# Attention and a routed mixture of experts on one core: the sums of k later, one of four probability copies on GpSimd, the pooled values' copy on ScalarE, and fewer copies for k's tail

## The chip, the cores and the metric

The kernel runs on one core of a Trainium2 chip. The metric is device time in microseconds (us): the median over runs of the kernel before is 694.59 us (three runs, 693.19 to 696.73). The engines named below are TensorE (PE in the profile, with its weight loads as PEld), VectorE (DVE), ScalarE (ACT), GpSimd (POOL) and SyncE (SP, which issues the plain loads and stores).

## The reference

Eight batches of eight heads, 576 positions of 64 numbers. Each head has two attentions that are added: a pooled one over sums of four neighbours (144 pooled positions), and a local one in which a position sees only those less than four away. The result, as 4,608 tokens of 512 numbers, goes through a router that picks one of eight experts for each token, and through that expert.

```python
q_d, k_d, v_d = (x.reshape(B, H, Sd, 4, D).mean(axis=3) for x in (q, k, v))
out_up = np.repeat(sm_attn(q_d, k_d, v_d), 4, axis=2)
mask = np.abs(pos[:, None] - pos[None, :]) < 4
attn = softmax(np.where(mask, scale * q @ k.T, -1e9))
x = rows_of(out_up + attn @ v)
logits = x @ w_gate + modality_bias[modality_id]
e = argmax(logits); gate = softmax(logits)[e]
out = gate * (relu(x @ w1[e]) @ w2[e])
```

The softmax's sums carry 1e-9 added.

## The kernel before

**Units.** Attention is cut into 32 units n, four to a batch; a unit is one pair of heads (g = n % 2 tells which half of a pair of units it is). Two units in sequence, an even and an odd one, share some work that is done once, with the even unit: the transposes of the last 64 positions of q and k (tpt), the pooled values (vp, vc), and the tails qT1, kT1 and kd1. So even units are the fuller ones. The steps of a unit, by the names that the text uses:

- tp (L275) and tpt (L288) transpose q and k on TensorE into PSUM. qT (L293, L295) and kT (L304, L305, L307) copy them on ScalarE into the tiles qT2 and kB, where kB has zeros around what belongs to the other head. kT1 are four copies of 64x64 for the tail of k.
- kd (L321, and L317 for the tail) sums four neighbours of k on VectorE, straight from the same PSUM tile that kT copies. qe and qd (L327, L331) do this for q on GpSimd in two steps.
- mk and sc (L341, L349) make the local scores on TensorE, window by window; lm and le (L356, L362) take their maxima and subtract them on VectorE; exp (L367) runs on ScalarE in place. scd (L376) makes the pooled scores, dm (L381) their maxima on VectorE, de (L389) their exponentials on ScalarE.
- z and zr (L393 to L399, VectorE) sum and invert; nl and nd (L403, L407, GpSimd) scale the two sets of probabilities.
- lt (L414, VectorE) transposes the local probabilities in blocks of 32; Pw_ (L419, ScalarE) copies them, in four copies of 32 partitions x 288 (Pw0 to Pw3), into a zeroed tile whose other columns stay zero. pdt (L428, TensorE) transposes the pooled ones and PdT (L436, ScalarE, two copies) takes them out of PSUM.
- vp makes the pooled values on TensorE and vc (L268) copies them on VectorE into the tile vd, once for two units. avd (L443) and avl (L458) are the products with the values, Od (L448, ScalarE) and X (L469, VectorE) scale and add them. For an odd batch, one copy on GpSimd (L1028) brings over the 64 positions left from the batch before it.

**Routing.** When the four units of batch b are through, its routing runs among the steps of unit 4b + 7: lg (L505), LT (L512) and lgt (L518) make the logits, L, ch1 and ch2 (VectorE, L524 to L555) find the expert, one-hot, and w is a small tile in that chain. pr (L570 to L574, TensorE) and pl turn it into places, which end in the tile si, and st (L615) scatters the tokens' numbers with GpSimd's indirect DMA, four scatters for an even batch and five for an odd one. For seven batches this lies in attention; the eighth is routed after it. In the last stretch of attention some weight preparation for the first expert joins in (whi L827, wlo L833).

**Order.** Nothing is reordered by a scheduler there. Each step has a number in the table PHASE, in units of one unit's time; a step of unit n is called at n + PHASE, steps of a batch at 4b + PHASE, and the sorted list of calls is emitted as it stands. So each engine's instructions are in that order, and each engine works through its own in turn, waiting where an operand isn't there. What two engines share is limited by PSUM tiles: the tag T (transposes tp, tpt, lgt, pdt, vp) has three buffers, S (scores) three, A (avl, avd, lg, pr) two.

**Experts.** From about 260 us on the experts' matmuls (L918, L966) run on TensorE, each f32 product made from three products of split numbers. Their order is set by a scheduler, and the eighth batch's routing lies at its beginning.

Of the kernel before, what the change touches and what calls it, by code (L numbers as in the profile page):

```python
# [7 lines left out]
F32 = mybir.dt.float32  # L8
# [14 lines left out]
SUB, WIN, KEYS = 24, 32, 30  # L23
BLK = 4 * SUB
NB = 6
PAD = 3
KT = S - SUB + WIN
# [17 lines left out]
NPW = 3  # L45
# [8 lines left out]

PHASE = {
# [22 lines left out]
class Consts:  # L78
    def __init__(s, tc, pool, psum):
        nc = tc.nc  # L80

        s.ps = psum
        pool.tile([128, 48], F32, name="pad")
        s.dummy = pool.tile([128, 128], BF16, name="dummy")
        nc.vector.memset(s.dummy, 0.0)
        s.busy(nc, 12)
        s.ident = pool.tile([128, 128], F32, name="ident")
        make_identity(nc, s.ident)
        s.identb = pool.tile([128, 128], BF16, name="identb")
        make_identity(nc, s.identb)  # L90

        x = pool.tile([128, 1], F32, name="warm")
        nc.vector.memset(x, 0.0)
        nc.scalar.activation(x, x, AF.Exp)
        m = pool.tile([128, WIN], BF16, name="band")
        nc.gpsimd.memset(m, 0.0)
        for j in range(4):
            t = m[32 * j : 32 * j + 32]
            nc.gpsimd.affine_select(out=t, in_=t, pattern=[[1, WIN]], compare_op=ALU.is_ge, fill=NEG, base=0,
                                    channel_multiplier=-1)  # L100
            nc.gpsimd.affine_select(out=t, in_=t, pattern=[[-1, WIN]], compare_op=ALU.is_ge, fill=NEG, base=6,
                                    channel_multiplier=1)
        s.mask = pool.tile([128, NB, WIN], BF16, name="mask")
        nc.vector.tensor_copy(s.mask, m.unsqueeze(1).broadcast_to([128, NB, WIN]))
        nc.vector.memset(s.mask[0:32, 0:2, 0:PAD], NEG)
        s.band = m

        s.pool = pool.tile([128, 32], F32, name="pool")
# [84 lines left out]
class Attention:  # L193


    def __init__(s, tc, ctx, ectx, C, psum, q, k, v):
        s.tc, s.C, s.ps = tc, C, psum
        nc = s.nc = tc.nc
        s.q, s.k, s.v = q, k, v

        s.ld = ectx.enter_context(tc.tile_pool(name="ald", bufs=2, side="right", reuse_waits="tile"))
        s.wk = ctx.enter_context(tc.tile_pool(name="awk", bufs=2, reuse_waits="tile"))
        s.one = ctx.enter_context(tc.tile_pool(name="aone", bufs=1, reuse_waits="tile"))
        s.QK, s.t = {}, {}
        s.vw = [(s.ld, s.one)[j].tile([128, H * NB, D], F32, name=f"vw{j}", bufs=1) for j in range(2)]

        s.qT2 = s.ld.tile([128, 2, S], F32, name="qT", bufs=1)
        s.kB = s.ld.tile([128, 2, 2, KT], F32, name="kT", bufs=1)
        nc.vector.memset(s.kB, 0.0)
        s.mask = s.one.tile([128, NB, WIN], BF16, name="mask")  # L210
        nc.vector.tensor_copy(s.mask, C.band.unsqueeze(1).broadcast_to([128, NB, WIN]))
        nc.vector.memset(s.mask[96:128, NB - 2 :, SUB + PAD : WIN], NEG)
        s.Pw = [s.one.tile([128, 2 * NB, 4, SUB], F32, name=f"Pw{j}") for j in range(NPW)]

        s.De = [s.one.tile([128, 3, 32 * NB], F32, name=f"de{j}") for j in range(3)]
        for j in range(2):
            (nc.vector, nc.gpsimd)[j].memset(s.vw[j], 0.0)

        for j in range(3):
            nc.vector.memset(s.De[j], 0.0)  # L220
# [44 lines left out]

    def vc(s, n, i):
        t = s.t["vd", n // 2] = s.wk.tile([96, 2, 4, D], F32, name="vd")
        s.nc.vector.tensor_copy(t, s.t.pop(("vp", n // 2)))  # L268

    def tp(s, n, nm):  # L270

# [25 lines left out]
    def kT_(s, n, i):  # L297
        g = n % 2
        p = s.t["tp", "t"][:, 1] if i else s.t["tp", "k", n]
        for a in range(2):  # L300
            r = slice(64 * a, 64 * a + 64)
            if i:
                t = s.kB[r].rearrange("m g a t -> m g (a t)")[:, :, KT * a + PAD : KT * a + PAD + 512 + 64]
                s.nc.scalar.copy(t[:, 0, 512:], p[r, :64])  # L304
                s.nc.scalar.copy(t[:, 1, :64], p[r, 64:])  # L305
            else:
                s.nc.scalar.copy(s.kB[r, g, a, PAD + 64 * g : PAD + 64 * g + 512], p[r])  # L307

# [107 lines left out]
    def Pw_(s, n, j):  # L416

        r = slice(32 * j, 32 * j + 32)
        s.nc.scalar.copy(s.Pw[n % NPW][r, :, j, :SUB], s.t["lt", n][r, :, :SUB])  # L419

    def pdt(s, n, i):

# [850 lines left out]
```

## Time and profile before

| | before |
|---|---|
| median of the runs (lowest, highest) | 694.59 us (693.19, 696.73; 3 runs) |
| profiled execution | 696.98 us: span 695.3, 1.7 around it |
| mean granted TensorE clock | 0.98 |
| TensorE busy | 649.5 us, 93% of the span |
| VectorE busy | 403.1 us, 58% |
| ScalarE busy | 379.9 us, 55% |
| GpSimd busy | 238.6 us, 34% |
| loads and stores (q1) | 86.71 MB, 53.9% of 16 DMA engines' span |
| GpSimd's indirect DMA (q0) | 19.18 MB, 8.6% |

The table's shares are averages over two different programs. Attention takes roughly the first 260 us of the span and keeps TensorE, VectorE, ScalarE and the DMA queues all well filled; the experts follow, and TensorE has no gap. In a row of the timeline the first number is the start in us from the beginning of the span, the second the duration in us, then engine, line, operation, output and inputs with their sizes; in square brackets is how long the engine sat idle before it and what ended that. Rows with x2 or x3 stand for so many instructions in a row. Instructions of one engine may overlap a little, the next one starting before the last one's record ends.

### The profile page before, as it was taken

The numbers are of one execution on the slowest core, as the hardware profiler recorded it, in microseconds if no ns is written. First come the engines' busy times: TensorE is split into PE (matmuls) and PEld (weight loads), VectorE is DVE, ScalarE is ACT, GpSimd is POOL, SyncE is SP. The second block draws the span as 40 slices with busy tenths as digits, with TensorE's granted clock in tenths as the row PEclk, the third lists the DMA queues.
The fourth block names the chain that finished last, engine by engine and source line by source line (L and its number), as shares of the span: only waits on it lengthen the run. The fifth ranks groups of instructions, "written<-read, shape, count | busy, mean of one in ns | idle before, by whom it ended". The sixth has DMA issues, their size and how long they took to land. (4 is left out here: it accounts for less than half of the span.)

```text
span 695.3 us, 16717 instructions
## 1 busy us (share of the span) xinstructions
PE 649.5 (93%) x6123; PEld 518.3 (75%) x6123; DVE 403.1 (58%) x938; ACT 379.9 (55%) x884; POOL 238.6 (34%) x302
## 2 busy tenths in 40 slices
PE   7898999888988889998999999999999999999896
PEld 4576666666656667886888888888888888889794
DVE  6688898888879886746444234323452343416610
ACT  4798998887888754452444334433443243425710
POOL 6644563635476564360220300403204012210111
PEclk9899999999999999999999999999999999999999
DMA  9899889998887938397561544616524345155700
GB/s 186 171 179 195 161 182 194 157 206 146 159 172 166 200 81 219 99 309 221 153 210 45 169 152 121 192 51 185 179 81 122 131 137 181 53 136 171 221 29 31
DMA packets 176423, 106.99 MB, mean 154 GB/s; under 512 B 136300, under 2 KB 154770, under 8 KB 176338
## 3 DMA queue, kind: packets, MB, share of 16 engines
q1 hardware_dynamic: 169138, 86.71, 53.9%
q0 software_dynamic: 7200, 19.18, 8.6%
q8 instruction: 50, 0.82, 0.5%
q14 instruction: 35, 0.29, 0.2%
HBM read 86.61 MB, written 19.51 MB: 153 GB/s over the span
## 5 line engine op out<-in xcount | busy, mean ns | idle before, releaser
L833 DVE TENSOR_TENSOR wlo<-raw,whi 128x1024 fp32r<-128x1024 f32 x73 | 87.9, 1227 | 79.6 <-ACT whi L827 72.4
L977 POOL DMA_INDIRECT out_dram<-o,tg x34 | 37.1, 1091 | 250.2 <-ACT o L969 194.6
L923 DVE SCALAR_TENSOR_TENSOR hl<-l,hh 128x512 fp32r<-128x512 f32 x72 | 49.5, 688 | 105.4 <-ACT hh L922 101.7
L922 ACT ACTIVATE hh<-l 128x512 fp32r<-128x512 f32 x72 | 42.6, 596 | 109.8 <-PE l L918 108.2
L966 PE MATMUL l<-whi,hh 128*128 128x512 f32 x256 | 100.2, 395 | 1.9 <-ACT hh L947 1.9
L966 PE MATMUL l<-whi,hl 128*128 128x512 f32 x256 | 99.9, 391 | 0.0
L966 PE MATMUL l<-wlo,hh 128*128 128x512 f32 x256 | 99.8, 391 | 0.0
L918 PE MATMUL l<-xh,whi 128*128 128x512 f32 (+1 forms) x256 | 95.1, 375 | 2.1 <-DVE hl L923 2.1
L918 PE MATMUL l<-xl,whi 128*128 128x512 f32 (+1 forms) x256 | 94.7, 370 | 0.0
L918 PE MATMUL l<-xh,wlo 128*128 128x512 f32 (+1 forms) x256 | 94.6, 370 | 0.0
L827 ACT CAST whi<-raw 128x1024 fp32r<-128x1024 f32 x70 | 71.5, 1051 | 29.6 <-DMA raw<-in_moe_w_dram 16.7
L969 ACT ACTIVATE o<-l,tg 128x512 f32<-128x512 f32 x37 | 25.4, 687 | 97.6 <-PE l L966 69.6
L403 POOL TENSOR_TENSOR le<-le,zr 128x384 f32<-128x384 f32 x32 | 26.6, 831 | 91.3 <-DVE zr L399 84.9
L966 PEld LDWEIGHTS l<-whi,hh 128*128 128x128 f32 x256 | 48.2, 188 | 11.8 <-ACT hh L947 2.2
L918 PEld LDWEIGHTS l<-xh,whi 128*128 128x128 f32 x256 | 48.1, 189 | 11.5 <-DVE hl L923 2.7
L419 ACT COPY Pw<-lt 32x288 f32<-32x288 f32 x128 | 54.5, 426 | 3.4 <-DVE lt L414 1.2
L966 PEld LDWEIGHTS l<-wlo,hh 128*128 128x128 f32 x256 | 48.2, 188 | 10.1
L966 PEld LDWEIGHTS l<-whi,hl 128*128 128x128 f32 x256 | 48.3, 189 | 9.5
L918 PEld LDWEIGHTS l<-xh,wlo 128*128 128x128 f32 x256 | 48.2, 188 | 8.3
L918 PEld LDWEIGHTS l<-xl,whi 128*128 128x128 f32 x256 | 48.3, 189 | 8.0
L896 DVE TENSOR_TENSOR xl<-xt,xh 128x512 fp32r<-128x512 f32 x37 | 24.3, 681 | 38.0 <-ACT xh L894 37.9
L615 POOL DMA_INDIRECT tab<-ig,si x36 | 38.5, 1068 | 20.7 <-DVE si L586 14.5
(245 smaller groups left out, 1297.7 us busy)
## 6 DMA issues: line engine op xcount, KB each, us to landing
raw<-in_moe_w_dram SPq DMA_DIRECT2D x176, 128.0 KB
raw<-in_moe_w_dram SPq DMA_DIRECT2D x44, 512.0 KB
vw<-in_v_dram SPq DMA_DIRECT2D x53, 180.0 KB
qt<-in_q_dram SPq DMA_DIRECT2D x30, 288.0 KB
kt<-in_k_dram SPq DMA_DIRECT2D x30, 288.0 KB
xs<-R SPq DMA_DIRECT2D x64, 128.0 KB
vw<-in_v_dram SPq DMA_DIRECT2D x15, 90.0 KB
xs<-R SPq DMA_DIRECT2D x12, 64.0 KB
```

The lines of the kernel that those rows point to most:

```text
L403: s.nc.gpsimd.tensor_tensor(e, e, z[:, : 2 * NB].unsqueeze(2).broadcast_to([128, 2 * NB, WIN]), op=ALU.mult)
L419: s.nc.scalar.copy(s.Pw[n % NPW][r, :, j, :SUB], s.t["lt", n][r, :, :SUB])
L615: i = nc.gpsimd.indirect_dma_start(out=s.tab[:, :], out_offset=bass.IndirectOffsetOnAxis(ap=C.si[:, t : t + 1], axis=0), in_=C.ig[:, t, :] ...
L827: (nc.gpsimd.tensor_copy if turn <= 4 else nc.scalar.copy)(hi, raw)
L833: (nc.gpsimd if turn == 4 else nc.vector).tensor_tensor(lo, raw, hi.bitcast(F32), op=ALU.subtract)
L896: nc.vector.tensor_tensor(xl[:, :, hs], p, xh[:, :, hs].bitcast(F32), op=ALU.subtract)
L918: nc.tensor.matmul(p[:, f % n, :], a[:, fs], x[:, k, :N], start=(k == 0 and i == 0), stop=(k == 3 and i == 2))
L922: nc.scalar.activation(hh[:, g, :N], p, AF.Relu)
L923: nc.vector.scalar_tensor_tensor(hl[:, g, :N], p, 0.0, hh[:, g, :N].bitcast(F32), op0=ALU.max, op1=ALU.subtract)
L966: nc.tensor.matmul(p, a[:, f, hs], x[:, f % 2, :], start=(f == 0 and i == 0), stop=(f == 7 and i == 2))
L969: nc.scalar.mul(o, p, T[:, h, 1:2].bitcast(F32))
L977: nc.gpsimd.indirect_dma_start(out=s.out[:, :], out_offset=bass.IndirectOffsetOnAxis(ap=T[:, h, 0:1], axis=0), in_=o, in_offset=None, boun ...
```

## The change

Four edits, all in attention:

1. kd0, the sums over the main 512 positions of k on VectorE, is called at phase 0.5095 in place of 0.3000. The steps between the two phases now come before it.
2. Of the four copies Pw_, the first (j = 0, partitions 0 to 31) is made by GpSimd, and it is called at 2.6300 in place of 2.7494: behind nd and, in the routing units, among the scatters.
3. vc, the copy of the pooled values out of PSUM, is made by ScalarE in place of VectorE, at 2.7495 in place of 2.6555.
4. The tail of k (kT1) takes two copies of 64x2x64 instead of four of 64x64. For that the tile kT becomes flat and 80 numbers longer, 2,416 a partition, so that the two halves of the tail lie at a constant distance; kB is a view of it, and its zeroing at the start is as much longer.

```diff
-    "kT1": 0.5356, "sc0": 0.5591, "qe": 0.6232, "qd": 0.6242, "lm0": 0.7343, "le0": 0.8414, "kd0": 0.3000, "kd1": 0.5400,
+    "kT1": 0.5356, "sc0": 0.5591, "qe": 0.6232, "qd": 0.6242, "lm0": 0.7343, "le0": 0.8414, "kd0": 0.5095, "kd1": 0.5400,
...
-    "nd": 2.5956, "vc": 2.6555, "Pw0": 2.7494, "pdt0": 2.7884, "PdT0": 2.9335, "PdT1": 2.9345,
+    "nd": 2.5956, "vc": 2.7495, "Pw0": 2.6300, "pdt0": 2.7884, "PdT0": 2.9335, "PdT1": 2.9345,
...
-        s.kB = s.ld.tile([128, 2, 2, KT], F32, name="kT", bufs=1)
-        nc.vector.memset(s.kB, 0.0)
+        s.kF = s.ld.tile([128, 4 * KT + 80], F32, name="kT", bufs=1)
+        nc.vector.memset(s.kF, 0.0)
+        s.kB = s.kF[:, : 4 * KT].rearrange("m (g a t) -> m g a t", g=2, a=2)
...
-        s.nc.vector.tensor_copy(t, s.t.pop(("vp", n // 2)))
+        s.nc.scalar.copy(t, s.t.pop(("vp", n // 2)))
...
-                t = s.kB[r].rearrange("m g a t -> m g (a t)")[:, :, KT * a + PAD : KT * a + PAD + 512 + 64]
-                s.nc.scalar.copy(t[:, 0, 512:], p[r, :64])
-                s.nc.scalar.copy(t[:, 1, :64], p[r, 64:])
+                t0, w = KT * a + PAD + 512, 2 * KT - 512
+                t = s.kF[r, t0 : t0 + 2 * w].rearrange("m (g t) -> m g t", g=2)
+                s.nc.scalar.copy(t[:, :, :64], p[r].rearrange("m (g t) -> m g t", g=2))
...
-        s.nc.scalar.copy(s.Pw[n % NPW][r, :, j, :SUB], s.t["lt", n][r, :, :SUB])
+        (s.nc.scalar.copy if j else s.nc.gpsimd.tensor_copy)(s.Pw[n % NPW][r, :, j, :SUB], s.t["lt", n][r, :, :SUB])
```

What each engine is given in its turn shows best side by side. The lines of the changed kernel are one higher from L210 on. VectorE in unit 7, the first with routing, before:

```order
L321 TENSOR_REDUCE kd<-tp 128x128
L356 TENSOR_REDUCE lm<-sc 128x6
L362 TENSOR_TENSOR le<-sc,lm 128x192
L524 TENSOR_REDUCE L<-lgt 128x16 x2
L531 TENSOR_TENSOR L<-L,tb 128x32
L533 TENSOR_REDUCE mx<-L 128x4
L534 TENSOR_TENSOR L<-L,mx 128x32
L414 STREAM_TRANSPOSE lt<-le 128x384
L381 TENSOR_REDUCE dm<-scd 128x3
L545 TENSOR_SCALAR w<-L 128x32
```

and now:

```order
L357 TENSOR_REDUCE lm<-sc 128x6
L363 TENSOR_TENSOR le<-sc,lm 128x192
L525 TENSOR_REDUCE L<-lgt 128x16 x2
L532 TENSOR_TENSOR L<-L,tb 128x32
L534 TENSOR_REDUCE mx<-L 128x4
L535 TENSOR_TENSOR L<-L,mx 128x32
L415 STREAM_TRANSPOSE lt<-le 128x384
L382 TENSOR_REDUCE dm<-scd 128x3
L322 TENSOR_REDUCE kd<-tp 128x128
L546 TENSOR_SCALAR w<-L 128x32
```

kd has moved from ahead of a score's maxima, past the logits, lt and dm, to a place just ahead of w. In units without routing it passes lm, le, lt and dm in the same way.

GpSimd in the second of the units that hold the scatters of batch 1, before (Pw_163 and the like are the three tiles that units take in turn, de_167 and de_168 those of the pooled probabilities):

```order
L615 DMA tab<-ig,si 41472x2
L407 TENSOR_TENSOR de_167<-de_167,zr 128x18x24
L327 TENSOR_TENSOR qe<-qT 128x288
L615 DMA tab<-ig,si 41472x2
L331 TENSOR_TENSOR qd<-qe 128x144
L615 DMA tab<-ig,si 41472x2
L403 TENSOR_TENSOR le<-le,zr 128x384
L615 DMA tab<-ig,si 41472x2
L407 TENSOR_TENSOR de_168<-de_168,zr 128x18x24
```

and now:

```order
L616 DMA tab<-ig,si 41472x2
L408 TENSOR_TENSOR de_167<-de_167,zr 128x18x24
L328 TENSOR_TENSOR qe<-qT 128x288
L616 DMA tab<-ig,si 41472x2
L332 TENSOR_TENSOR qd<-qe 128x144
L420 COPY Pw_164<-lt 32x12x24
L616 DMA tab<-ig,si 41472x2
L404 TENSOR_TENSOR le<-le,zr 128x384
L616 DMA tab<-ig,si 41472x2
L408 TENSOR_TENSOR de_168<-de_168,zr 128x18x24
```

One copy has come in, behind qd and ahead of two scatters, le and de.

ScalarE in an even unit, before:

```order
L293 ACTIVATE qT<-tpt 128x128
L448 ACTIVATE Od<-avd 128x144
L304 COPY kT<-tpt 64x64
L305 COPY kT<-tpt 64x64
L304 COPY kT<-tpt 64x64
L305 COPY kT<-tpt 64x64
L367 ACTIVATE le<-le 128x384
L419 COPY Pw_165<-lt 32x12x24
L389 ACTIVATE de_166,z<-scd,dm 128x6x24 x3
L436 COPY PdT<-pdt 96x2x144 x2
```

and now:

```order
L294 ACTIVATE qT<-tpt 128x128
L449 ACTIVATE Od<-avd 128x144
L306 COPY kT<-tpt 64x2x64 x2
L368 ACTIVATE le<-le 128x384
L269 COPY vd<-vp 96x512
L390 ACTIVATE de_166,z<-scd,dm 128x6x24 x3
L437 COPY PdT<-pdt 96x2x144 x2
```

The four small copies are two, and where Pw0 stood, the copy of the pooled values stands. In an odd unit Pw0's place is empty. TensorE's order doesn't change.

## The prediction

> **What bounds the kernel now.** I began with busy times by stage (the windows view), since an average over the whole run would mix two programs. Columns: the stretch, its length, then busy time of TensorE, its weight loads, VectorE, ScalarE, GpSimd, granted clock, DMA share, GB/s.
>
> ```profile
> 180.00:200.00 20.00, 18.87 (x396) 14.38 (x396) 18.54 (x58) 18.89 (x62) 12.40 (x16) 1.00 0.87 163
> 160.00:165.00 5.00, 2.84 (x65) 2.25 (x65) 4.97 (x13) 2.47 (x9) 4.55 (x6) 1.00 1.02 129
> 165.00:170.00 5.00, 4.41 (x51) 2.59 (x51) 4.33 (x17) 4.05 (x11) 2.59 (x4) 0.66 0.91 166
> 219.50:224.10 4.60, 3.87 (x95) 2.88 (x92) 4.39 (x13) 4.33 (x12) 4.17 (x7) 1.00 0.63 63
> 400.00:500.00 100.00, 100.00 (x458) 82.92 (x457) 39.55 (x45) 38.59 (x53) 19.36 (x18) 1.00 0.50 153
> ```
>
> In 400 to 500 us, the experts, TensorE is busy 100.00 of 100, so nothing the change does to other engines can shorten that stage; but what attention gains or loses moves all of it, whole. In 180 to 200, attention, TensorE, ScalarE and VectorE are each busy over 18.5 of 20: three engines share the bound. So the waits come next, over 40 to 245 us: engine and line, what they waited for, us in total, times, longest.
>
> ```profile
> POOL le L403 <- DVE zr L399: 73.8, 20, 8.2
> DVE kd L321 <- ACT kT L307: 13.0, 12, 2.2
> ...
> PE pdt L428 <- POOL de L407: 5.4, 8, 1.9
> ...
> PE tp L275 <- ACT PdT L436: 3.4, 8, 1.4
> ...
> ACT le L367 <- DVE le L362: 2.9, 3, 1.2
> PE avl L458 <- ACT Pw L419: 2.6, 5, 0.6
> ```
>
> TensorE waits little: for ScalarE 3.4 + 2.6 = 6.0 us, for GpSimd 5.4. The first two rows are idle time of engines that are not late. The timeline tells which engine closes the ring of a unit. Here is an odd unit without routing, ScalarE, then TensorE (start, duration, engine, line, operation).
>
> ```profile
> 67.91 0.69 ACT L436 COPY PdT<-pdt 96x288 f32<-96x288 f32 x2 [0.18 <-ACT de L389]
> ...
> 69.11 1.18 ACT L307 COPY kT<-tp 64x512 f32<-64x512 f32 x2
> 70.31 1.31 ACT L419 COPY Pw<-lt 32x288 f32<-32x288 f32 x3
> ...
> 72.39 0.41 ACT L419 COPY Pw<-lt 32x288 f32<-32x288 f32 x1
> ...
> 73.91 0.69 ACT L436 COPY PdT<-pdt 96x288 f32<-96x288 f32 x2
> ```
> ```profile
> 71.67 1.21 PE L458 MATMUL avl<-Pw,vw 128*64 128x96 f32 x24 [0.59 <-issue]
> ...
> 73.28 0.54 PE L428 MATMUL pdt<-ident,de 64*96 64x64 f32 x12
> ```
>
> From PdT to PdT it is 6.0 us, and the ring runs PdT, qT, kT, three Pw copies, then TensorE's avl, sc, pdt, which ends at 73.82, and PdT again at 73.91. The Pw0 copy at 72.39 lies beside TensorE's part. In an even unit ScalarE has no gap at all:
>
> ```profile
> 122.00 0.20 ACT L304 COPY kT<-tpt 64x64 f32<-64x64 f32 x1
> ...
> 122.67 0.52 ACT L367 ACTIVATE le<-le 128x384 f32<-128x384 f32 x1
> 123.10 0.42 ACT L419 COPY Pw<-lt 32x288 f32<-32x288 f32 x1
> 123.53 0.38 ACT L389 ACTIVATE de<-scd,dm 128x144 f32<-128x144 f32 x1
> ...
> 124.61 0.69 ACT L436 COPY PdT<-pdt 96x288 f32<-96x288 f32 x2
> ```
>
> **The change, part by part.** Prices first: busy time and mean ns of the groups, then the one GpSimd copy of the trace.
>
> ```profile
> L307 ACT COPY kT<-tp 64x512 f32<-64x512 f32 x64 | 37.0, 578 | 1.0
> ...
> L321 DVE TENSOR_REDUCE kd<-tp 128x128 f32<-128x512 f32 x32 | 21.5, 671 | 17.1 <-ACT kT L307 17.0
> ...
> L293 ACT ACTIVATE qT<-tpt 128x128 f32<-128x128 f32 x16 | 4.4, 277 | 2.4 <-PE tpt L288 2.0
> ...
> L1028 POOL COPY X<-late 128x256 f32<-128x256 f32 x4 | 1.6, 395 | 0.0
> ```
>
> *Even units, ScalarE.* Pw0 leaves: 123.53 - 123.10 = 0.43 off. The vd copy (96x512) comes: the kT copy, also 512 wide out of PSUM, lasts 0.578, and two follow each other in 1.18 (69.11), so I take 0.59. The four small kT copies took 122.67 - 122.00 = 0.67; two copies of 64x128 replace them, nearest to qT's 0.277 each. Those two kT copies, to different partition halves, did not overlap, so I take 0.57 for both, 0.10 off. Sum +0.59 - 0.43 - 0.10 = +0.06 a unit, x 16 = +0.96. If the new copies overlapped as well as the old (0.36 for two) it would be -0.15 a unit; if they saved nothing, +0.16: -2.4 to +2.6.
>
> *Odd units, ScalarE.* Pw0's 0.4 goes, but TensorE's pdt still ends at 73.82, so PdT can start only 73.91 - 73.82 = 0.09 earlier; and for the handing over I leave 0.03 of it: 0.06. Nine odd units carry no routing (16 less 7): -0.54. This is where most of the change's apparent gain stays behind.
>
> *The sums of k (kd), VectorE.* They move from ahead of a unit's score maxima to behind dm. 17.1 us of idle stood before them, most of it for kT, but VectorE's wait is no one's end except where something late is queued behind it: in the three places where ScalarE's exp waits for le (2.9 us) kd's 0.67 no longer stands ahead; I credit 3 x 0.65 = -1.95, bounds 0 and -2.9. In the seven units that carry a batch's routing the new place is worse. VectorE, then TensorE and ScalarE, of the first:
>
> ```profile
> 55.84 0.69 DVE L321 TENSOR_REDUCE kd<-tp 128x128 f32<-128x512 f32 x1 [1.25 <-ACT kT L307]
> ...
> 57.10 0.34 DVE L524 TENSOR_REDUCE L<-lgt 128x16 f32<-128x64 f32 x2
> ...
> 58.53 0.57 DVE L381 TENSOR_REDUCE dm<-scd 128x3 f32<-128x432 f32 x1
> 59.02 0.16 DVE L545 TENSOR_SCALAR w<-L 128x32 f32<-128x32 f32 x1
> ```
> ```profile
> 56.25 0.44 PE L518 MATMUL lgt<-ident,LT 128*128 128x128 f32 x2 [0.88 <-ACT LT L512]
> ...
> 60.72 0.18 PE L570 MATMUL pr<-oh,tri 128*128 128x32 bf16 x1 [0.43 <-DVE X L469]
> ```
> ```profile
> 61.62 0.60 ACT L295 ACTIVATE qT<-tp 128x512 f32<-128x512 f32 x1 [0.55 <-PE tp L275]
> ```
>
> From dm on the chain is tight: w, then X; TensorE's pr has waited 0.43 for X, its transposes (tp) follow, and ScalarE's qT has waited 0.55 for those. kd inside this chain costs 0.65. What it gives back ahead: L could start when lgt ends, 56.69, plus a handing over, near 56.8 instead of 57.10, so 0.3. Net +0.35, x 7 = +2.45; bounds 0.3 and 0.65, +2.1 to +4.5.
>
> In even units kd also stands before the small sums (L317), whose buffer the next pdt takes. I price it at nothing, because ScalarE has no gap there until 124.61; without that cover it would be up to 0.2 a unit.
>
> *Pw0 on GpSimd.* By elements, 395 x 288 / 256 = 0.44 us; no row shows a copy on 32 partitions. Pw0 waits for lt, and behind it stand the routing scatters and the next nl. Where GpSimd idles, that costs nothing: nl (L403) waits for zr,
>
> ```profile
> 69.80 0.83 POOL L403 TENSOR_TENSOR le<-le,zr 128x384 f32<-128x384 f32 x1 [0.66 <-ACT kT L307]
> ...
> 126.80 0.83 POOL L403 TENSOR_TENSOR le<-le,zr 128x384 f32<-128x384 f32 x1 [0.85 <-DVE zr L399]
> ```
>
> 0.66 to 0.85, about 0.75, even beside scatters, in the four even batches. In an odd batch (1, 3, 5) with its five scatters, the second unit's chain has no slack:
>
> ```profile
> 224.17 0.54 PE L428 MATMUL pdt<-ident,de 64*96 64x64 f32 x12 [0.22 <-POOL de L407]
> ```
>
> From 219.5 to 224.1 (first table) GpSimd is busy 4.17 of 4.60 in seven instructions one behind the other, two of them scatters, and TensorE's pdt waits for the last of them, de. Pw0 slips in between and is paid in full, 3 x 0.44 = +1.32. The other side: up to 1.05 each, the second rival.
>
> The Trainium skill speaks against this part ("GPSIMD Engine Reference", section 1, Specifications): GpSimd shares its SBUF interfaces with VectorE, and contends with VectorE instructions that have two SBUF inputs. The trace bears it out once (two pieces of the timeline, then all 32 qe: shortest, median, longest ns):
>
> ```profile
> 232.47 1.56 DVE L833 TENSOR_TENSOR wlo<-raw,whi 128x1024 fp32r<-128x1024 f32 x1
> ...
> 232.91 1.64 POOL L327 TENSOR_TENSOR qe<-qT 128x288 f32<-128x288 f32 x1
> ```
> ```profile
> L327 POOL TENSOR_TENSOR qe<-qT x32: 662/666/1641, 10.7 to 237.3; 128x288 f32<-128x288 f32 x32
> ```
>
> By that rule a Pw0 that met such an instruction would be stretched too, which is the second rival's time; by the median of qe, which is within 0.01 of the shortest, the sum's 1.32 stands.
>
> *Sum.* +0.96 - 0.54 - 1.95 + 2.45 + 1.32 = +2.2. The profiled execution, 696.98 (695.3 of span), becomes 699.2; it lies 2.4 above the median of 694.59, which becomes 696.8.
>
> **The rivals.** *ScalarE alone sets the pace, and the change is faster.* Over a pair of units ScalarE sheds 2 x 0.43 + 0.10 and takes 0.59, net -0.37, x 16 = -5.9; about as much as TensorE's waits for ScalarE, 6.0, which would all go: 694.6 - 6.0 = 688.6. For it: ScalarE's 18.89 of 20 and its gapless even unit. Against it: pdt's end at 73.82 in the odd ring, and VectorE's 18.54. Chance 0.25.
>
> *GpSimd's copy is slow, and the change is slower.* The qe above took 1.64 against 0.67 elsewhere when it ran beside VectorE's two-input wlo, 2.46 times as long. At that ratio Pw0 takes 0.44 x 2.4 = 1.05. Odd batches pay 3 x 1.05, and the four even ones what exceeds their slack, 4 x (1.05 - 0.75): 3.15 + 1.2 = 4.35 in place of 1.32, sum +5.3, so 699.9. It decides from about 0.8 us per copy, where 0.9 + 3p + 4(p - 0.75) passes 3.5. For it: this row. Against it: only one of 32 qe was stretched so. Chance 0.15.
>
> *The clock.* In 160 to 165 TensorE was busy 2.84 of 5, and in the next 5 us it was granted 0.66, which cost (1 - 0.66) x 5 = 1.7. The moved waits can add such a dip or remove one: 2.2 + 1.7 or 2.2 - 1.7, 698.5 or 695.1. Chance 0.10.
> By the Trainium skill ("TensorE: Matmul & The Clock Gate", Part 1, The HAM clock gate) the clock falls only after an idle window of about 3.4 us; by that no dip could come here, and this rival would be nothing. The trace does not agree: the dip follows 5 us that were more than half busy.
>
> **How the numbers follow.** The forecast has 0.50. A change of under 0.5% (3.5 us) is about what a measurement of this kernel can't tell from none. Faster by more, below 691.1: nearly all of the first rival and a little of the forecast's low tail, 0.24. Slower by more, above 698.1: of the second rival 0.13, of the clock 0.04, and of the forecast 0.12, since its terms reach from -2.4 to +2.6 on ScalarE and to +4.5 on VectorE; 0.29. The same: 0.47. The range goes up to 700.5, past the second rival, leaving 0.04 above. Down to 689.5 it takes in a third of the first rival, leaving 0.16 below: together 0.20.
>
> **What would show it.** Right: in odd units pdt still ends just before PdT, and TensorE's waits for PdT stay near 3; the vd copy shows 0.59 on ScalarE, the new kT copies 0.28, Pw0 on GpSimd 0.44; in routing units pr's wait for X grows by about 0.35; in odd batches pdt waits longer for GpSimd's de. Wrong: the waits for PdT and Pw fall near zero and the attention stage ends 5 us sooner (first rival), or Pw0 on GpSimd lasts over 0.8 (second).

## The result and the profile after

| | before | after |
|---|---|---|
| median (lowest, highest; runs) | 695.74 us (691.58, 698.22; 9) | 698.81 us (695.95, 703.52; 9) |
| ratio to before, 95% interval | | 1.0065 [1.0038, 1.0092] |
| profiled execution (span) | 696.98 us (695.3) | 697.65 us (696.0) |

The ratio is +4.5 us on 695.7, with an interval of +2.6 to +6.4 (the two medians lie 3.1 apart); the forecast was +2.2. The two profiled spans lie only 0.7 apart, in part because the clock dipped four times between 160 and 660 us in before's and once in after's; so they are compared below stage by stage.

Attention first. The waits from 40 to 245 us in the changed kernel (us in total, times, longest):

```profile
POOL le L404 <- DVE zr L400: 54.9, 15, 6.8
...
PE pdt L429 <- POOL de L408: 7.5, 8, 3.2
...
PE lgt L519 <- ACT LT L513: 6.3, 7, 1.1
...
PE pr L571 <- DVE X L470: 3.2, 4, 0.8
...
ACT le L368 <- DVE le L363: 3.1, 3, 2.3
PE avl L459 <- ACT Pw L420: 3.1, 5, 0.7
...
PE pr L571 <- DVE late L470: 2.8, 3, 0.9
...
PE tp L276 <- ACT PdT L437: 0.3, 1, 0.3
```

and three of the kernel before:

```profile
PE lgt L518 <- ACT LT L512: 5.2, 6, 0.9
...
PE pr L570 <- DVE X L469: 1.7, 4, 0.4
...
PE pr L570 <- DVE late L469: 1.4, 3, 0.5
```

VectorE's wait of 13.0 us with kd on kT is gone from the list: kd now comes so late that kT is always there. TensorE's wait for PdT fell from 3.4 to 0.3, and yet attention is not shorter, as the units below show. pr's waits for X and late together rose from 3.1 to 6.0 over seven routings, 0.41 each. The prices, by line:

```profile
L420 POOL COPY Pw<-lt 32x288 f32<-32x288 f32 x32 | 14.4, 449 | 8.4 <-DVE lt L415 8.3
L269 ACT COPY vd<-vp 96x512 f32<-96x512 f32 x16 | 9.3, 580 | 0.7 <-PE vp L264 0.4
L306 ACT COPY kT<-tpt 64x128 f32<-64x128 f32 x32 | 8.2, 258 | 0.4
```

What a unit costs is best read from one mark. "Ring n" is here the time from the first PdT copy (L436, L437 in the timeline) of unit n - 1 to that of unit n. Where nothing near it was changed, a ring repeats to within 0.02 us from kernel to kernel (ring 13 is 7.87 or 7.88 in all fourteen profiles), unless a clock dip or a gap falls into it in which TensorE waited for nothing that the profile shows; so a few hundredths are real. In us (e1 and so on are the experiments below):

| ring | before | after | Pw0 alone (e3) | vd alone (e6) | kd alone (e8) | after, kd early in routing units (e2) | after, four tail copies (e12) |
|---|---|---|---|---|---|---|---|
| 8 (even; 12, 16 alike) | 6.70 | 6.76 | 6.42 | 7.18 | 6.70 | 6.76 | 6.88 |
| 9 (odd) | 8.20 | 8.20 | 8.20 | 8.20 | 8.20 | 8.20 | 8.20 |
| 11 (odd batch) | 6.18 | 6.74 | 6.56 | 6.00 | 6.32 | 6.74 | 6.74 |
| 14 (routing) | 7.23 | 7.66 | 7.26 | 7.71 | 7.70 | 7.37 | 7.76 |
| 19 | 8.90 | 6.99 | 8.91 | 8.04 | 7.48 | 6.98 | 7.00 |
| 22 (routing) | 7.23 | 7.66 | 7.27 | 7.54 | 7.60 | 7.37 | 7.77 |

Rings 6 to 27 add up to 159.65 us before and 160.65 after, +1.0 (each from a profile in which it was undisturbed: before or e1; after, and for 23 to 25 e2). As profiled the sums are 164.86 and 163.85: a clock dip and several such gaps fall into before's, a gap of 1.65 us into after's, and they fall elsewhere in other executions. So the +1.0 rests on that choice of profiles. Units 28 to 31 are not in that sum: there GpSimd's whi waits for a weight load, 1.8 us before and 2.2 after, but 0.9 in e2, and that moves from one execution to the next.

The experts are the other place. VectorE at their beginning, before and then after; si holds the places of the last batch's tokens, and GpSimd's scatters wait for it:

```profile
281.58 0.19 DVE L585 TENSOR_REDUCE sf<-sl 128x5 f32<-128x40 f32 x1
281.85 1.23 DVE L833 TENSOR_TENSOR wlo<-raw,whi 128x1024 fp32r<-128x1024 f32 x1
...
283.22 0.16 DVE L586 CAST si<-sf 128x5 int32<-128x5 f32 x1
284.16 1.22 DVE L833 TENSOR_TENSOR whl<-raw,whl 128x1024 fp32r<-128x1024 f32 x1 [0.79 <-issue]
285.31 0.68 DVE L923 SCALAR_TENSOR_TENSOR hl<-l,hh 128x512 fp32r<-128x512 f32 x1
```
```profile
281.82 0.19 DVE L586 TENSOR_REDUCE sf<-sl 128x5 f32<-128x40 f32 x1
282.83 1.23 DVE L834 TENSOR_TENSOR whl<-raw,whl 128x1024 fp32r<-128x1024 f32 x1 [0.82 <-ACT whl L828]
...
284.20 0.68 DVE L924 SCALAR_TENSOR_TENSOR hl<-l,hh 128x512 fp32r<-128x512 f32 x1
284.80 0.16 DVE L587 CAST si<-sf 128x5 int32<-128x5 f32 x1
```

The scheduler has put whl and hl ahead of si. The first expert's matmuls began at 258.10 before and at 256.09 after, so si went from 25.1 to 28.7 us behind them. In all kernels with this order TensorE's and ScalarE's turn with VectorE's: the four transposes xt behind lgt come 11.2 us after the first matmul before (269.30) and, with 12 of the expert's matmuls now ahead of them, 14.5 after (270.56); on ScalarE an hh now stands ahead of a whi. So "order" below means all three together; no run here separates them. Also, the first scatter behind si now lasts twice as long, begun 0.14 us after a whl on VectorE (285.10), where before it began 0.51 us ahead of one:

```profile
283.65 1.03 POOL L615 DMA_INDIRECT tab<-ig,si  x1 [14.50 <-DVE si L586]
```
```profile
285.24 2.12 POOL L616 DMA_INDIRECT tab<-ig,si  x1 [17.37 <-DVE mn L749]
```

Behind si stand the five scatters, then the gathers (xg) and a store of results (out_dram) in GpSimd's queue; that store frees a buffer "o" for which VectorE waits, by after's row, at the head of its queue, with a weight product (wlo) behind it. GpSimd and VectorE before:

```profile
302.57 1.31 POOL L977 DMA_INDIRECT out_dram<-o,tg  x1 [0.30 <-issue]
```
```profile
310.05 0.42 DVE L652 TENSOR_TENSOR o<-ltri,mn 128x256 f32<-128x256 f32 x1 [4.45 <-issue]
310.51 0.42 DVE L654 TENSOR_REDUCE mincl<-o 128x16 f32<-128x256 f32 x1
310.85 1.21 DVE L833 TENSOR_TENSOR wlo<-raw,whi 128x1024 fp32r<-128x1024 f32 x1
```

and after:

```profile
305.81 1.04 POOL L978 DMA_INDIRECT out_dram<-o,tg  x1 [0.30 <-ACT whi L828]
```
```profile
314.06 0.43 DVE L653 TENSOR_TENSOR o<-ltri,mn 128x256 f32<-128x256 f32 x1 [6.99 <-DMA out_dram<-o,tg]
...
315.63 1.22 DVE L834 TENSOR_TENSOR wlo<-raw,whi 128x1024 fp32r<-128x1024 f32 x1
...
318.12 0.69 DVE L924 SCALAR_TENSOR_TENSOR hl<-l,hh 128x512 fp32r<-128x512 f32 x1
318.72 0.14 DVE L769 TENSOR_SCALAR rcnt<-rcnt 128x1 f32<-128x1 f32 x1
```

So wlo lies 52.8 us behind the first matmul before, and 59.5 after. For before's o the profile names no releaser. TensorE waits at that place; after's long wait is put down to rcnt, which follows the hl of 318.12 on VectorE. TensorE's idle time from 295 to 326 us, before and after,

```profile
319.05 0.50 PE L918 MATMUL l<-xh,whi 128*128 128x512 f32 x1 [0.47 <-DVE hl L923]
...
323.88 0.50 PE L918 MATMUL l<-xh,whi 128*128 128x512 f32 x1 [1.59 <-DVE hl L923]
```
```profile
312.20 0.50 PE L919 MATMUL l<-xh,whi 128*128 128x512 f32 x1 [0.91 <-ACT whi L828]
...
318.86 0.52 PE L919 MATMUL l<-xh,whi 128*128 128x512 f32 x1 [3.26 <-DVE rcnt L769]
```

is 2.1 and 4.2 us, and right behind the longer wait the clock falls (the second row: 3.4 us at 0.50, worth 1.7):

```profile
300.00:325.00 25.00, 20.83 (x87) 16.61 (x86) 12.88 (x21) 11.88 (x15) 11.69 (x11) 0.93 1.04 307
319.20:322.60 3.40, 3.40 (x10) 2.63 (x9) 1.89 (x3) 0.90 (x2) 0.00 (x0) 0.50 1.02 307
```

### The profile page after: what moved, and what is told of

It is laid out like the page before. It is cut to its first block, busy times and chain, and to the rows that moved or that the text cites. A ratio compares the mean times of both kernels' runs of the same rounds, so it can differ in the third digit from the quotient of the medians.

```text
span 696.0 us, 16656 instructions
## 1 busy us (share of the span) xinstructions
PE 641.6 (92%) x6123; PEld 512.7 (74%) x6123; DVE 394.4 (57%) x922; ACT 374.8 (54%) x836; POOL 251.8 (36%) x334
## 5 line engine op out<-in xcount | busy, mean ns | idle before, releaser
L970 ACT ACTIVATE o<-l,tg 128x512 f32<-128x512 f32 x37 | 25.3, 686 | 97.7 <-PE l L967 62.4
L404 POOL TENSOR_TENSOR le<-le,zr 128x384 f32<-128x384 f32 x32 | 26.6, 831 | 67.5 <-DVE zr L400 61.5
L459 PE MATMUL avl<-Pw,vw 128*64 128x96 f32 x768 | 39.2, 250 | 6.4 <-ACT Pw L420 3.8
```

The lines of the kernel that those rows point to most:

```text
L404: s.nc.gpsimd.tensor_tensor(e, e, z[:, : 2 * NB].unsqueeze(2).broadcast_to([128, 2 * NB, WIN]), op=ALU.mult)
L459: s.nc.tensor.matmul(p[64 * a : 64 * a + 64, c], vw[:, NB * (4 * (hp // 2) + hp % 2 + 2 * a) + k, :], Pw[:, 2 * k + a], start=True, stop=T ...
L970: nc.scalar.mul(o, p, T[:, h, 1:2].bitcast(F32))
```

## The experiments

Ratios are to runs of before on the same chip, with their 95% interval; 1% is 6.9 us. Theory A came out of the two traces: about half of the loss is in the experts, through the order that the scheduler chose there. The order turned out to be fickle: kd's move alone gives it, vd's move alone gives it, Pw0 and the tail copies don't, and even kd late in the single unit 5 does.

**e1: before, with the experts in the order of after.**

```diff
-                        call(n + p, values if f == "X" else getattr(at, parts.get(f, f)), n, i)
+                        call(n + (0.5095 if nm == "kd0" and n == 5 else p), values if f == "X" else getattr(at, parts.get(f, f)), n, i)
```

> The kernel before, with kd later in unit 5 alone. In attention that touches one unit, but it turns the scheduler's order on VectorE at the start of the experts into the one that the changed kernel has: the cast to si (the places of the last batch's tokens) comes behind one more weight product (whl) and one more hl. Theory A (about half of the change's loss lies in the experts, by this order): si and the scatters behind it come 2 to 4 us later against the first expert's matmuls, TensorE's gap near 319 us grows from 2.1 to about 4, and the time is 2 us above before. Rival B (all of the loss lies in attention): si moves, but the gap and the time stay as before, within 0.5 us.

1.0041 [1.0012, 1.0070], +2.8 us. si came 27.4 us behind the first matmul, and TensorE's waits from 295 to 325 us were 4.6:

```profile
PE l L918 <- DVE rcnt L768: 3.1, 1, 3.1
PE l L918 <- DVE hl L923: 1.0, 1, 1.0
PE l L918 <- ACT o L969: 0.5, 1, 0.5
```

Attention's rings are before's, the routing and odd-batch ones too. So that order costs by itself, and rival B falls.

**e2: after, with kd early in the routing units.** In after's call line:

```diff
+                        call(n + (0.3 if nm == "kd0" and n % 4 == 3 and n > 4 else p), ...
```

> The changed kernel, with kd back at its old phase in the seven routing units alone; that also gives the experts before's order on VectorE. Theory A: pr's waits for X fall from 6.0 back to about 3, worth 1.7 to 2.4 us, and the experts give back another 2 us: the time is that of before plus 0 to 1 us. Rival B (the loss is Pw0 on GpSimd and vd on ScalarE): it stays 3 us or more above before. Rival C (only the routing units count): 2 us above before.

0.9986 [0.9955, 1.0018], -1.0 us: the whole loss is gone. Rings 6, 10, 14, 18, 22, 26, 30 are shorter than after's by 0.30, 0.48, 0.29, 0.47, 0.29, 0.05 and 0.20, 2.1 in all; si is at 25.3 and TensorE's waits near 310 to 320 us are 0.9. It undoes both things at once, so it doesn't tell them apart; e5 does. pr's waits are 4.0 in all, against 6.0 in after and 3.1 in before.

**e3 and e4: before, with Pw0 on GpSimd; and with the two tail copies as well.** The edits are those of the change, alone.

> The kernel before, with Pw0 on GpSimd alone; the experts keep before's order. By the prediction's steps ScalarE sheds 0.43 us in each of 16 even units, where it has no gap, 0.06 in the odd ones, and GpSimd takes 1.3 in the odd batches: -6.9 - 0.5 + 1.3 = -6, so 0.9 % faster. Rival D (VectorE closes the even unit as well as ScalarE): even units gain under 0.1 each, and with 1.3 for GpSimd the time is that of before or 1 us above.

> The kernel before, with Pw0 on GpSimd and two copies for k's tail; vd stays on VectorE, kd early, the experts in before's order. By the prediction's steps another 0.10 x 16 = 1.6 off: 7.5 us below before, 1.1 % faster. Rival D (VectorE closes the even unit too): no more than 1 us off.

0.9988 [0.9962, 1.0014] and 0.9991 [0.9958, 1.0025]. The even ring fell by 0.28 (6.70 to 6.42), not by 0.43, and the tail copies took nothing more off it; routing rings and odd rings didn't move; rings 11 and 27 grew by 0.39 each, ring 3 by 0.2 to 0.3. What is gained in some even units goes into GpSimd's chain and into the start. Rival D was half right: something else closes the even unit after 0.28.

**e5: after, with kd early in the even units**, which gives the experts before's order and leaves the routing units as in after (`n % 2 == 0` in e2's line).

> The changed kernel, with kd back at its old phase in the even units; in all odd units, the routing ones among them, it stays late. That gives the experts before's order on VectorE, and leaves the rest of the change as it is. Theory A: the experts' 2 to 3 us go (si about 25 us behind the first expert's matmul instead of 28.7, TensorE's gaps near 311 to 319 us about 2 instead of 4), attention keeps its loss: about 1.5 us above before. Rival C (the routing units carry all of the loss): as slow as the changed kernel, 4 us above before.

0.9994 [0.9965, 1.0023], -0.4 us. Ring 14 and ring 22 are after's, 7.66 both, and ring 11 6.57; rings 10, 18 and 26 are 0.2 to 0.7 longer than after's, ring 19 0.3 shorter; TensorE's only wait from 295 to 325 us is 1.0:

```profile
PE l L919 <- DVE hl L924: 1.0, 1, 1.0
```

So an attention no shorter than after's, with before's order in the experts, is as fast as before, within -2.4 to +1.6 us: rival C falls, and theory A stands, perhaps with more in the experts than I had put there.

**e6: before, with vd's copy on ScalarE alone.**

> The kernel before, with vd's copy on ScalarE alone; the experts take the changed kernel's order. By the prediction's price ScalarE gains 0.59 in each even unit, where it has no gap: rings of units 8, 12, 16, 20 go from 6.70 to 7.29, +9 us in all with the experts' 2 to 3 beside it, so about 12 us above before. If VectorE closes those units as well (the rings fell by 0.28 only, to 6.42, when Pw0's 0.43 left ScalarE), the ring goes up by less than 0.59, since VectorE is spared 0.67.

1.0055 [1.0021, 1.0089], +3.8 us, a third of what was expected. Even ring +0.48, near the price; but ring 19 -0.9 and rings 11 and 27 -0.2 and -0.3, where VectorE is spared 0.67. Its experts have after's order, with waits of 3.2. The parts do not add up here: as profiled its rings 6 to 27 are 4.0 us longer than before's, and with e1's 2.8 that makes 6.8, above the interval's 6.2.

**e7: Pw0 on GpSimd, two tail copies, kd late in four units, on top of before**, chosen so that the experts keep before's order.

```diff
+                        call(n + (0.5095 if nm == "kd0" and n in (20, 21, 22, 25) else p), ...
```

> The kernel before, with Pw0 on GpSimd, two copies for k's tail, and kd late in units 20, 21, 22 and 25 alone; vd on VectorE, before's order in the experts. What the rings say of the parts: even units 8, 12, 16, 20, 24 at 6.42 instead of 6.70 (-0.28 each), the ring of unit 19 at 7.0 instead of 8.9 if a late kd in units 20 to 22 is what frees VectorE there (-1.9), rings 3, 11 and 27 longer by 0.3 to 0.4 each: 2 to 3 us below before, 0.4 % faster. Rival: the ring of unit 19 stays at 8.9, since it was kd in other units, and the time is that of before.

0.9948 [0.9916, 0.9980], -3.6 us [-5.8, -1.4]: faster than both kernels. Even rings 6.42, ring 19 7.69. As profiled, its rings 6 to 27 give only 1.2 of that.

**e8: before, with kd late in all units alone.**

> The kernel before, with kd late in all units alone. Theory A: the ring of unit 19 falls from 8.9 to 7.0, the rings of units 6, 10, 14, 18, 22 grow by 0.3 to 0.5 each (the routing chain), and the experts lose 2 to 3 by their order: 2 to 3 us above before. Rival B (the experts' order costs nothing): before's time, within 0.5 us.

1.0070 [1.0037, 1.0103], +4.8 us. Ring 19 is 1.4 shorter, the routing rings 0.3 to 0.6 longer, and in the experts TensorE waits 3.9. Here the parts add up: rings 6 to 27 are 1.8 longer, and with e1's 2.8 that makes 4.6.

**e9: after, with si made on GpSimd for the last batch.**

```diff
-        nc.vector.tensor_copy(C.si[:, t0 : t0 + G], sf)
+        (nc.vector if b < B - 1 else nc.gpsimd).tensor_copy(C.si[:, t0 : t0 + G], sf)
```

> The changed kernel, with one cast moved: for the last batch, si is made by GpSimd, which uses it next, instead of VectorE. Attention and VectorE's order stay as in the changed kernel, without si. Theory A: si no longer stands behind whl and hl, comes about 2 us sooner (about 26.5 us behind the first expert's matmul instead of 28.7), TensorE's gaps at 310 to 320 us fall from 4 to about 2, and most of the experts' 2 us is back: 1.5 to 3 us below the changed kernel, 1.5 to 3 above before. Rival B' (another part of the new order costs it, such as the weight products that stand later): gaps and time stay as in the changed kernel, 4.5 above before.

1.0060 [1.0037, 1.0083]: no gain that can be told from after. The trace shows half of the chain mended: si at 26.0 instead of 28.7, wlo at 56.5 instead of 59.5, TensorE's wait 2.5 instead of 4.2,

```profile
PE l L919 <- DVE rcnt L769: 2.5, 1, 2.5
```

but the first two scatters took 2.0 us each, each begun just behind a whl on VectorE, and the clock dipped there all the same. So the place of si is a part of it, and that it is the whole was not shown; sf itself, and the weight products around it, stand otherwise in that order too.

**e10: e7 with e9's edit.**

> The kernel of e7_mix, with the same cast on GpSimd. There si already stood early on VectorE, so theory A expects little: the time of e7_mix within 1 us, 3 to 4 below before.

0.9972 [0.9945, 1.0000]: between e7 and before, with waits of 3.4 near 310 to 320 us for which I have no cause, si being early. Long waits and a slow kernel don't go together here. The cast on GpSimd helped neither kernel.

**e11: e7, with kd late in units 18 to 21 instead**, which turns the experts' order.

> The kernel of e7_mix, with kd late in units 18 to 21 instead of 20, 21, 22 and 25. Attention is nearly the same (the ring of unit 19 at 7.0 to 7.7), but the experts have the changed kernel's order on VectorE. Theory A: 2 us slower than e7_mix, 1 to 2 below before. Rival B: as e7_mix.

1.0021 [0.9995, 1.0048], some 5 us slower than e7 where 2 were expected, and slower than before: waits of 3.8 and a dip at 314 us in the experts.

**e12: after, with four tail copies.**

> The changed kernel with before's four small copies for k's tail. By the prediction's price ScalarE has 0.10 more in each even unit, and the rings of units 8, 12, 16, 20, 24 go from 6.76 to 6.86: 1 to 1.6 us slower than the changed kernel. If the two copies save nothing (beside Pw0's going they changed no ring: 6.42 with and without them), the rings and the time stay.

1.0116 [1.0071, 1.0161] of six runs, by the ratios 3.5 us above after, with a wide interval. Its rings say what of that is the copies: 6.88 instead of 6.76, and 7.76 instead of 7.66.

**All of them together.** TensorE's idle time in the experts' first stretch (295 to 326 us), and the time from the first to the last matmul of the experts, in the profiles:

| order in the experts | kernels | ratio to before | si, us behind first matmul | TensorE idle, us | clock dip at 314 to 320 us | first to last matmul, us |
|---|---|---|---|---|---|---|
| before's | before, e2, e3, e4, e5, e7 | 0.9948 to 1 | 25.1 to 26.6 | 0.9 to 2.1, mean 1.4 | 1 of 6 | 427.9 to 431.9, mean 430.0 |
| after's | after, e1, e6, e8, e11, e12 | 1.0021 to 1.0116 | 27.2 to 29.1 | 3.2 to 4.6, mean 3.9 | 5 of 6 | 431.0 to 434.9, mean 432.8 |
| before's, si on GpSimd | e10 | 0.9972 | 24.3 | 3.4 | 0 of 1 | 431.4 |
| after's, si on GpSimd | e9 | 1.0060 | 26.0 | 2.5 | 1 of 1 | 432.6 |

That the order costs time is shown: e1 has it with attention's rings unchanged, and all six ratios of the second row lie above those of the first, though the intervals of single kernels touch. By which step it costs it is not shown: the chain from si to wlo is read from the traces, and e9, which moved si, mended the waits in part and the time by nothing that can be told from none.

## Why the prediction was right in sign and half in size

*What failed.* The step "nothing the change does to other engines can shorten that stage; but what attention gains or loses moves all of it, whole". It was read from 400 to 500 us, where TensorE is busy 100.00 of 100. From 300 to 325 it is not: two waits, 2.1 us together, stood in before's own trace (a third, of 1.9, at 657 us), so the remark further up that TensorE has no gap in the experts was wrong as well. The change lengthened them, not by work but by the order in which the scheduler emitted it. That is 2.5 us of waiting (3.9 - 1.4), and a clock dip worth 1.7 in four more of six profiles; from the first to the last matmul the stage is 2.8 us longer, six profiles against six, with some overlap between the groups. e1 has it alone, at +2.8 [+0.8, +4.8].

*Attention* was forecast at +2.2; its rings 6 to 27 measure +1.0, and what units 28 to 31 add could not be told from their weight loads. Term by term:

- Even units, +0.06 each: 6.70 to 6.76, as forecast. But it is made of +0.48 for vd (e6), -0.3 for Pw0 (e3, or e6 to e12) and -0.12 for the tail (e12 to after), where I had +0.59, -0.43 and -0.10: the errors cancel, which is luck. vd's copy lasts the 0.58 that was priced, but the next instruction, de, begins 0.48 behind its start (77.87 and 78.35), so the records overlap by 0.10; the price came from two kT copies that did not overlap. kd ahead of the small sums costs nothing there, as priced: 6.70 with kd alone (e8).
- Odd units, -0.06 each: 0.00 in rings 9, 13, 17 and 21. Nothing of Pw0's going is left there. The reason stands (another engine ends the ring), the remnant did not come.
- The credit of -1.95 for kd and le: -1.91, but all of it in ring 19, and not in three places; kd alone gives 1.4 of it, vd alone 0.9. There the tables for the first experts fill VectorE (third number of busy time in before's window of ring 19):

```profile
156.25:165.15 8.90, 6.01 (x118) 4.66 (x118) 8.73 (x30) 5.93 (x20) 6.88 (x9) 1.00 0.94 143
```

  ScalarE's waits for le did not go, 2.9 before and 3.1 after. The size was right by luck.
- Routing units, +0.35 each: +0.41 in pr's wait for X, and +2.1 over seven rings (e2) where 2.45 was forecast. VectorE, TensorE and ScalarE of the first one:

```profile
55.26 0.36 DVE L525 TENSOR_REDUCE L<-lgt 128x16 f32<-128x64 f32 x2 [0.91 <-PE lgt L519]
...
56.79 0.61 DVE L382 TENSOR_REDUCE dm<-scd 128x3 f32<-128x432 f32 x1
57.32 0.68 DVE L322 TENSOR_REDUCE kd<-tp 128x128 f32<-128x512 f32 x1
57.92 0.17 DVE L546 TENSOR_SCALAR w<-L 128x32 f32<-128x32 f32 x1
...
59.12 0.82 DVE L470 TENSOR_TENSOR X<-avl,Od 128x288 f32<-128x288 f32 x2
```
```profile
59.63 0.18 PE L571 MATMUL pr<-oh,tri 128*128 128x32 bf16 x1 [0.80 <-DVE X L470]
```
```profile
60.53 0.60 ACT L296 ACTIVATE qT<-tp 128x512 f32<-128x512 f32 x1 [0.93 <-PE tp L276]
```

  VectorE now idles 0.91 ahead of L, kd sits between dm and w, and pr (0.43 to 0.80) and qT (0.55 to 0.93) wait 0.37 and 0.38 longer: the forecast chain.
- Pw0 on GpSimd, 3 x 0.44: it takes 0.41 (0.413 median of 32), and rings 11 and 27 grow by 0.39 with it alone (by 0.14 and 0.09 more with a late kd, by e8). The remaining place is ring 19, where VectorE was later anyway and Pw0 cost nothing (8.90 and 8.91). So 0.8 of 1.3. GpSimd in the chain that the prediction showed, and TensorE behind it:

```profile
217.12 0.44 POOL L332 TENSOR_TENSOR qd<-qe 128x144 f32<-128x144 f32 x1
217.50 0.43 POOL L420 COPY Pw<-lt 32x288 f32<-32x288 f32 x1
...
221.16 0.92 POOL L408 TENSOR_TENSOR de<-de,zr 128x432 f32<-128x432 f32 x1
```
```profile
222.13 0.54 PE L429 MATMUL pdt<-ident,de 64*96 64x64 f32 x12 [0.63 <-POOL de L408]
```

*The rivals.* ScalarE alone (first rival): its sign in the profile came, TensorE's wait for PdT fell to 0.3, and the time did not follow. I had named that wait's stay near 3 as a mark of being right; it was a bad mark, since TensorE then waits for other things: from 40 to 245 us its waits for LT rose from 5.2 to 6.3, those for de from 5.4 to 7.5. The 5.2 for LT, ScalarE's work too, was left out of the 6.0 us that the prediction gave as TensorE's waits for ScalarE. What decides is ring 9 and its like, which did not move with Pw0. GpSimd's slow copy (second): one of 32 Pw0 took 1.47 us, beside the same wlo that stretched a qe to 1.64 before, and the rest 0.41; the stretch changed its victim and cost nothing new. The clock (third): it was there, but in the experts, behind the new wait.

## What to carry to other kernels

Where a scheduler orders the next stage, any edit upstream can turn its order: compare the whole order before and after, on every engine, and not only around the edit. A stage that is full on its busiest engine in one window can still wait elsewhere; look at its waits, its beginning above all, before calling it rigid. And a mark per unit, such as the start of one copy, shows 0.06 us where total times need dozens of runs to show 2.

## What the hardware showed unexpectedly

The clock dips at the experts' beginning came with TensorE's waits. Where the longest single wait was 3.1 to 3.9 us, the clock fell at its end in five kernels of six; where it was 0.8 to 1.8, in one of six; with e9's 2.5 it fell too, with e10's 2.0 it did not. Each dip is a stretch of 3.4 us at 0.50. By the Trainium skill ("TensorE: Matmul & The Clock Gate", Part 1, The HAM clock gate) 3.4 us is the length of the gate's window, and the clock falls after an idle one. The length agrees; that a whole window must be idle does not, since the dip came behind waits of 2.5 and 1.8 us too (e9, e4). In the 3.4 us ahead of the seven dips TensorE was busy for 5 to 48%; e10's 43% (310.0 to 313.4 us) brought none.

GpSimd's indirect DMAs were stretched by one kind of neighbour. Of the 1,652 in the fourteen profiles 74 took over 1.7 us, and each of these began within 0.42 us after the start of one of VectorE's 128x1024 products of two tiles (wlo, whl; 1.2 us each). The 1,370 during which no such product ran took at most 1.19 us. The scatters of the result section and of e9 are among the 74.

At 161.68 us before, and at the same place after, stands one VectorE operation of 128x2:

```profile
161.68 1.31 DVE L682 SCALAR_TENSOR_TENSOR er<-uf,er 128x2 f32<-128x2 f32 x1
```
```profile
159.09 0.15 DVE L683 SCALAR_TENSOR_TENSOR er<-uf,er 128x2 f32<-128x2 f32 x1
```

Before, it ends at 162.99, and GpSimd's scaling of de (162.04, 0.92 long) had ended at 162.96. So GpSimd may hold up VectorE as well as the other way round; that was seen here once and not tried.
